# Two linear attentions behind a gate: B queries of the last two tiles moved into the key part, kv fed two tiles at a time, zeros on TensorE at the start, W buffers in another order

## The chip, the cores and the metric

One Trainium2 chip, one core of it. The metric is the device time of one execution in microseconds (us), as the median of several executions. TensorE is PE in the profile, with its weight loads in a row of their own (PEld); VectorE is DVE, ScalarE is ACT, GpSimd is POOL, and SP issues the DMAs.

## What is computed

Both attentions read the same x (2048 rows of 576), with 32 heads of 18 columns. A uses elu-like features, B a learned map per head and two softmaxes over 18 columns; neither is causal. A gate per row mixes the two.

```python
def reference(A_x, A_wqkv, A_wo, B_x, B_wqkv, B_w_phi, B_wo, gate_w):
    x = A_x
    g = sigmoid((x * gate_w).sum(-1, keepdims=True))
    # A: q, k, v from x @ A_wqkv, phi(t) = where(t > 0, t + 1, exp(t)) + 1e-6
    #    kv = einsum("bhsd,bhse->bhde", phi(k), v);  z = phi(k) summed over s
    #    a  = (phi(q) kv) / (phi(q) z + 1e-6) @ A_wo
    # B: q, k, v from x @ B_wqkv, pq = q w_phi per head, pk = k w_phi per head
    #    phi_q = concat([softmax(pq), softmax(-pq)]), phi_k likewise, then as in A with B_wo
    return g * a + (1 - g) * b
```

All is f32. The kernel keeps that accuracy by splitting each operand into a high and a low part in fp32r and multiplying three of the four products.

## The kernel before

The 2048 rows are 16 tiles of 128. A projection of a tile (`proj`, L157) is 14 matmuls of 288 columns for each half of the 576 columns: 4 full k-tiles with three products each, and the last 64 rows with their low parts packed into two matmuls. Results go to two-bank PSUM tiles named pq or to one-bank tiles named tr, two buffers of each name. Two more banks, named bk, hold the sums kv[0] and kv[1] over all key tiles, and later the output sums.

The work runs in four parts.

- Loads and folding of weights. A weight takes one of five W buffers; raw pieces come by DMA through wraw buffers (and, at the start, uw ones), ACT rounds them to the high part (L115) and DVE or POOL makes the low part (L117). The per-head map of B is folded into its key and query weights (`fold_w`, L142).
- The key part, over tiles 0 to 15: v of A (`do_v`), k of A with its feature map (`do_ak`, L173 to L175), k of B with its two softmaxes (`do_bk`: maximum and minimum L180 and L181, subtractions L187 and L188, exponential L189, sums L191, scaling L198), v of B, and the sums kv (L212): 11 small matmuls of A and 11 of B for each tile, fed with the features of the tile before. v stands in two buffers (vo).
- The transition: kv is masked into tiles (kt), z is summed out of it (L520 for B), A's kv is multiplied with A's output weight into MA (L348, L351, evacuated at L354), and B's kv is placed into kb_h and kb_l (L533, L537). Into this are woven the query units of tiles 14 and 15.
- The query loop, in blocks of two tiles in the order 14, 15, 0 to 13. For a tile, `q_units` projects B's query (the softmax steps as in `do_bk`, without the scaling), then A's with two gate columns more (L173 to L175, and gg = 1 + exp(-+gate), L366), then `norm_a` (L371 to L377) and `norm_b` (L384 to L392, scaling L198) apply denominators and gate; `tr_units` transposes the features (L428, L435, L440, L442) and splits them (L423, L424); `num` multiplies B's features with kb (L460, split at L465); `out_units` makes the output (L490).

The order of instructions on each engine isn't that of the code: a scheduler with a timeline of its own moves them, within the limits set by data and buffers. Each engine then takes its list strictly in order. All loads and stores wait in one list, on SP.

Of the kernel before, what the change touches and what calls it, by code (L numbers as in the profile page):

```python
# [1 line left out]

# [12 lines left out]
P = 128  # L15
# [13 lines left out]
def tile_gated_mix(ctx, tc, xT, wAk, wAv, wBv, wAq, wkT, wqT, phi, woA, woB, out):  # L29
# [68 lines left out]
    def load_x(t, eng=G):  # L98
        raw = wk.tile([P, 640], F32, name="xraw")
        nc.sync.dma_start(raw, xT[t].rearrange("p j n -> p (j n)"))  # L100
        raw = raw.rearrange("p (j n) -> p j n", n=P)
        xh = wk.tile([P, KT, P], F32R, name="xh")
        xl = wk.tile([P, KT, P], F32R, name="xl")
        A.activation(xh, raw, AF.Copy)  # L104
        eng.tensor_tensor(xl, raw, r(xh), op=ALU.subtract)  # L105
        return xh, xl
# [91 lines left out]
        eng.tensor_tensor(u3, u3, rs[:, :, None].to_broadcast([P, 64, DH]), op=ALU.mult)  # L198
# [102 lines left out]
    kv_b(t0, u0)
# [9 lines left out]
    for k in range(2):
        pz = tr_tile()
        w = min(324, D - 324 * k)
        for i in range(3):
            n = min(108, w - 108 * i)
            PE.matmul(pz[:, 108 * i:108 * i + n], sel_z, kta[3 * k + i][:, P:P + n], start=True, stop=True)
        A.activation(z_a[:, 324 * k:324 * k + w], pz[:, :w], AF.Copy)

    WoB = w_tile()
    for g in range(4):
        split(woB[:, g, :], WoB[:126, g, :D], WoB[:126, 5 + g, :D], G)
    raw = wraw_tile()[:96, :D]
    nc.sync.dma_start(raw, woB[:96, 4, :])
    A.activation(WoB[:64, 4, :D], raw[:64], AF.Copy)
    A.activation(wob_y[:64], raw[:64], AF.Copy)
    A.activation(wob_y[64:96], raw[64:96], AF.Copy, scale=tcol[64:96])
    G.tensor_tensor(wob_x[:96], raw[:96], r(wob_y[:96]), op=ALU.subtract)
    MA = w_tile()  # L330
# [30 lines left out]
    def maps_a(pa):  # L361
        f = phi_elu(pa)
        gg = sm.tile([P, 2], F32, name="gg")
        for i, sgn in enumerate((-1.0, 1.0)):
            A.activation(gg[:, i:i + 1], pa[:, 1, HB:HB + 1], AF.Exp, scale=sgn)
        V.tensor_scalar(gg, gg, 1.0, None, op0=ALU.add)  # L366
# [28 lines left out]

    qs = {}

    def q_units(t, x=None):
        x = x or load_x(t)
# [16 lines left out]
    def tr_units(t, at, uwt, tiles=(tr_tile, tr_tile)):
        f, uw = qs.pop(t)
# [81 lines left out]
        while seqs:  # L499
            seqs = [s for s in seqs if next(s, "end") != "end"]  # L500

    qu0, qu1, mau = q_units(t0, x0), q_units(t1, x1), ma_units()
    for _ in range(2):
        next(qu0)
    kv_b(t1, u1)


    for p, kt in enumerate(ktb):
        b, o = b_region(p)
        for a, m, n in widths(p):  # L510
            rows, c = slice(64 * a, 64 * a + m), P + 54 * a
            V.tensor_tensor(kt[rows].rearrange("p (s c) -> p s c", s=2)[:, :, c:c + n],
                            kv[b][rows, o:o + 2 * n].rearrange("p (s c) -> p s c", s=2),
                            mask[rows, a, None, :n].to_broadcast([m, 2, n]), op=ALU.mult)
        if p % 2 == 0:
            pz = tr_tile()
        n = min(108, D - 108 * p)
        for s in range(2):
            o = 216 * s + 108 * (p % 2)
            PE.matmul(pz[:, o:o + n], sel_z, kt[:, 320 * s + P:320 * s + P + n], start=True, stop=True)  # L520
# [3 lines left out]
        if p == 0:  # L524
            continue
        g, nh = GROUPS[p - 1]
        n, w = nh * DH, (nh * DH if g < 4 else 80)
        pk = tr_tile()
        for s in range(2):
            for c0, c1, base in [(0, n, 0)] + ([(72, 80, 64)] if g == 4 else []):  # L530
                for q in (g, p):
                    off = P + 126 * g - 108 * q
                    PE.matmul(pk[:n, 126 * s + c0:126 * s + c1], ktb[q][:, 320 * s + off:320 * s + off + n],  # L533
                              place[:, off + base:off + base + c1 - c0], start=(q == g), stop=(q == p))
        pkv = pk[:n, :252].rearrange("p (s c) -> p s c", s=2)[:, :, :w]
        A.activation(kb_h[:n, 2 * g:2 * g + 2, :w], pkv, AF.Copy)
        V.tensor_tensor(kb_l[:n, 2 * g:2 * g + 2, :w], pkv, r(kb_h[:n, 2 * g:2 * g + 2, :w]), op=ALU.subtract)  # L537
# [93 lines left out]
```

## Time and profile before

| | us |
|---|---|
| median of 3 executions | 625.88 (625.6 to 626.61) |
| the profiled execution | 623.18 |
| its span (first to last instruction) | 621.5 |

Busy time in the profiled execution, share of the span and instructions:

```profile
PE 604.0 (97%) x5000; PEld 591.5 (95%) x5000; DVE 391.5 (63%) x644; ACT 204.7 (33%) x420; POOL 174.4 (28%) x126
```

The median lies 2.7 us above the profiled execution; changes are counted on the profile and then carried over to the median. Rows of a timeline give the start, the time from there to the end, the engine, the line, the operation, output<-inputs and the number of records; a wait and what ended it stand in brackets. Ends of matmuls are modelled and overlap, so that pace is read from starts. An fp32 matmul leaves two records, an fp32r one leaves one. Rows of groups give the busy us of the group, the mean ns of one, and the idle us ahead of it.

### The profile page before, as it was taken

What the parts mean: (1) busy time and instruction counts of PE and PEld (TensorE: products, weight loads), DVE (VectorE), ACT (ScalarE), POOL (GpSimd) and SP (SyncE); (2) the same over time, 40 slices, a digit from 0 to 9 for tenths busy, and PEclk for the clock granted to TensorE, in tenths of its full rate; (3) what the DMA queues carried; (4) which work ended last, traced back from release to release, by engine and by line L of the source; (5) the groups of instructions that cost most, each with busy time, mean ns of one, the idle gap of its engine ahead of it and who ended that gap; (6) DMA issues with size and microseconds to landing.
All of it is one profiled execution on the core that took longest, in us unless ns stands there. A gap on an engine that the chain in (4) does not pass through costs nothing.

```text
span 621.5 us, 11676 instructions
## 1 busy us (share of the span) xinstructions
PE 604.0 (97%) x5000; PEld 591.5 (95%) x5000; DVE 391.5 (63%) x644; ACT 204.7 (33%) x420; POOL 174.4 (28%) x126
## 2 busy tenths in 40 slices
PE   6999999999999999999998799999999999999997
PEld 6999999999999999999997599999999999999997
DVE  6373353323323332326999998989889988889920
ACT  6342232221222222235333344243332334332331
POOL 6013221112222222245245212434133443312300
PEclk9999999999999999999999999999999999999999
DMA  8441130000000000024011101011010110000001
GB/s 285 124 142 41 44 112 3 21 22 22 22 22 24 22 22 24 22 64 122 22 38 50 35 22 40 22 42 41 20 41 22 41 42 20 20 20 20 16 24 39
DMA packets 12660, 27.94 MB, mean 45 GB/s; under 512 B 1388, under 2 KB 1388, under 8 KB 12608
## 3 DMA queue, kind: packets, MB, share of 16 engines
q1 hardware_dynamic: 12608, 27.19, 14.1%
q8 instruction: 39, 0.64, 0.4%
q14 instruction: 13, 0.11, 0.1%
HBM read 22.47 MB, written 4.72 MB: 44 GB/s over the span
## 4 chain that ended last, share of the span: by engine, by line
PE 82%; DVE 13%; ACT 2%; DMA 2%; issue 1%; SPq 0%; ACTq 0%
PE pq L157 32%; PE tr L157 19%; PE bk L490 16%; PE bk L212 5%; PE tr L460 4%; PE tr L435 2%; DVE row L384 1%; DVE dd L385 1%; DMA wraw<-wBv 1%; DVE uw L198 1%; PE tr L428 1%; DVE W L424 1%; PE pq L142 1%; DVE gg L366 1%; DVE row L175 1%; DVE den L373 1%
## 5 line engine op out<-in xcount | busy, mean ns | idle before, releaser
L157 PE MATMUL pq<-W,xh 128*128 128x288 f32 (+1 forms) x1152 | 254.3, 300 | 0.2 <-DVE den L390 0.2
L157 PEld LDWEIGHTS pq<-W,xh 128*128 128x128 f32 x1152 | 190.9, 189 | 3.1 <-PE tr L348 0.6
L157 PE MATMUL pq<-W,xl 128*128 128x288 f32 (+1 forms) x640 | 187.1, 298 | 0.0
L157 PE MATMUL tr<-W,xh 128*128 128x288 f32 x576 | 124.4, 301 | 5.8 <-ACT W L115 5.3
L105 POOL TENSOR_TENSOR xl<-xraw,xh 128x640 fp32r<-128x640 f32 x29 | 45.4, 1566 | 301.2 <-ACT xh L104 300.6
L157 PEld LDWEIGHTS pq<-W,xl 128*128 128x128 f32 x640 | 120.8, 189 | 0.2
L157 PEld LDWEIGHTS tr<-W,xh 128*128 128x128 f32 x576 | 96.7, 193 | 6.6 <-ACT W L115 5.3
L157 PE MATMUL tr<-W,xl 128*128 128x288 f32 x320 | 93.9, 299 | 0.0
L174 DVE TENSOR_SCALAR row<-row 128x576 f32<-128x576 f32 x32 | 24.4, 762 | 101.2 <-ACT row L173 101.2
L233 ACT ACTIVATE vo<-tr 128x288 f32<-128x288 f32 x64 | 25.9, 407 | 150.2 <-PE tr L157 150.2
L490 PE MATMUL bk<-W,ath 128*128 128x288 f32 x288 | 63.5, 301 | 1.1 <-ACT ath L423 0.7
L191 DVE TENSOR_REDUCE ss<-uw 128x64 f32<-128x1152 f32 x32 | 43.2, 1351 | 31.0 <-ACT uw L189 30.9
L157 PEld LDWEIGHTS tr<-W,xl 128*128 128x128 f32 x320 | 61.8, 193 | 0.0
L490 PE MATMUL bk<-W,vo 126*128 126x288 f32 x384 | 61.3, 299 | 0.0
L490 PEld LDWEIGHTS bk<-W,vo 126*128 126x128 f32 x384 | 54.0, 189 | 0.0
L180 DVE TENSOR_REDUCE mm<-pq 128x32 f32<-128x576 f32 x32 | 23.9, 748 | 47.0 <-PE pq L157 47.0
L189 ACT ACTIVATE uw<-uw 128x1152 f32<-128x1152 f32 x32 | 37.3, 1167 | 41.7 <-DVE uw L188 41.0
L490 PEld LDWEIGHTS bk<-W,ath 128*128 128x128 f32 x288 | 47.2, 189 | 1.5 <-ACT ath L423 0.9
L490 PE MATMUL bk<-W,atl 128*128 128x288 f32 x160 | 47.4, 297 | 0.0
L371 POOL TENSOR_TENSOR row<-row,z_a 128x576 f32<-128x576 f32 x16 | 30.1, 1882 | 52.5 <-DVE row L175 52.5
L460 PE MATMUL tr<-W,kb_h 126*126 126x256 f32 (+1 forms) x160 | 32.4, 283 | 1.0 <-DVE vo L465 0.8
L198 POOL TENSOR_TENSOR uw<-uw,rs 128x1152 f32<-128x1152 f32 x15 | 32.3, 2155 | 0.7 <-DVE rs L193 0.7
(138 smaller groups left out, 875.7 us busy)
## 6 DMA issues: line engine op xcount, KB each, us to landing
xraw<-xT SPq DMA_DIRECT2D x30, 320.0 KB, 3.1
out<-row SPq DMA_DIRECT2D x16, 288.0 KB, 2.1
wraw<-woA SPq DMA_DIRECT2D x6, 288.0 KB, 2.9
wraw<-wAq SPq DMA_DIRECT2D x5, 289.0 KB
wraw<-wBv SPq DMA_DIRECT2D x5, 288.0 KB, 4.2
wraw<-wkT SPq DMA_DIRECT2D x4, 315.0 KB
wraw<-wqT SPq DMA_DIRECT2D x4, 315.0 KB
uw<-wAk SPq DMA_DIRECT2D x4, 288.0 KB
```

The source lines that it names most:

```text
L105: eng.tensor_tensor(xl, raw, r(xh), op=ALU.subtract)
L157: PE.matmul(dst, xx[:, j, :], W[:, w, c0:c0 + n], start=(i == 0), stop=(i == len(steps) - 1))
L174: V.tensor_scalar(fx, fx, 1.0, EPS, op0=ALU.min, op1=ALU.add)
L180: V.tensor_reduce(mm[:, :32], heads(pq), op=ALU.max, axis=AX.X)
L189: A.activation(uw, uw, AF.Exp)
L191: V.tensor_reduce(ss, uw.rearrange("p s (h d) -> p (s h) d", d=DH), op=ALU.add, axis=AX.X)
L198: eng.tensor_tensor(u3, u3, rs[:, :, None].to_broadcast([P, 64, DH]), op=ALU.mult)
L212: PE.matmul(dst, vt[t % 2][:, which, 3 * gr:3 * gr + nh, :].rearrange("p h d -> p (h d)"), rhs, start=(t == 0 and first), stop=(t == NT - ...
L233: A.activation(vt[t % 2][:, which, 16 * hf:16 * hf + 16, :DH], pv[:, :HB].rearrange("p (h d) -> p h d", d=DH), AF.Copy)
L371: G.tensor_tensor(zw, f[:, :D], z_a, op=ALU.mult)
L460: PE.matmul(dst, kk[:n, i, :w], uu[:n, i, :256], start=(m == 0), stop=(m == 5))
L490: PE.matmul(po[:, :HB], l, w, start=(i == 0), stop=(i == len(steps) - 1))
```

## The change

It has five parts.

1. At the very start, DVE sets 128x288 elements to zero, and PE multiplies them five times in fp32, into a bk bank that nothing reads.
2. v stands in four buffers (two named ath, two vo), and `kv_pair` feeds kv with two tiles at once: A of both, then B of both, at every even tile.
3. B's query projection and softmax of tiles 14 and 15 (`q_b`) are taken out of `q_units` and put into the key part; their `norm_b` follows after both A queries. `fold_a` is the former code as a function, B's kv is folded in two loops instead of one, and the kt tiles are made later. The first two units of MA are woven with tile 15's `q_b`.
4. gg + 1 is done by ACT instead of DVE; tile 15's key scaling of B by POOL instead of DVE.
5. MA takes its W buffer ahead of WoB, so that MA gets the one that WAk leaves and WoB that of WBk.

```diff
+    warm = row_tile()[:, :HB]
+    V.memset(warm, 0.0)
+    pw = bank_tile()
+    for _ in range(5):
+        PE.matmul(pw[:, :HB], warm[:, :P], warm, start=True, stop=True)
...
-    for i in range(2):
-        v = wk.tile([P, 2, H, VC], F32, name="vo")
+    for i in range(4):
+        if i < 2:
+            v = wk.tile([P, 2, 640], F32, name="ath").rearrange("p a c -> p (a c)")[:, :2 * H * VC]
+            v = v.rearrange("p (a h d) -> p a h d", a=2, d=VC)
+        else:
+            v = wk.tile([P, 2, H, VC], F32, name="vo")
...
+    def kv_pair(pend):
+        for t, f, _ in pend:
+            kv_a(t, f)
+        for t, _, u in pend:
+            kv_b(t, u)
+        pend.clear()
...
-        if pend[0] is not None:
-            kv_a(t - 1, pend[0])
-        kv_b(t - 1, pend[1])
+        if t % 2 == 0:
+            kv_pair(pend)
...
-        V.tensor_scalar(gg, gg, 1.0, None, op0=ALU.add)
+        A.activation(gg, gg, AF.Copy, bias=1.0)
...
-    qu0, qu1, mau = q_units(t0, x0), q_units(t1, x1), ma_units()
-    for _ in range(2):
-        next(qu0)
+    do_v(t0, x0, WAv, 0)
+    f0 = do_ak(x0)
+    kv_pair(pend)
...
+    u0 = do_bk(x0)
+    do_v(t0, x0, WBv, 1)
+    weave(q_b(t0, x0, qb))
+    do_v(t1, x1, WAv, 0)
+    f1 = do_ak(x1)
+    kv_a(t0, f0)
+    kv_b(t0, u0)
...
+    WAq = load_w(wAq, 578, G)
+    u1 = do_bk(x1)
+    kv_a(t1, f1)
+    fold_a()
+    MA = w_tile()
+    WoB = w_tile()
...
+    mau = ma_units()
+    do_v(t1, x1, WBv, 1)
+    weave(q_b(t1, x1, qb), islice(mau, 2))
     kv_b(t1, u1)
...
-    weave(qu0, mau)
-    weave(qu1)
+    weave(mau, q_a(t0, x0, qa), q_a(t1, x1, qa))
+    for t in (t0, t1):
+        norm_b(*qb[t], qa[t][1])
+        qs[t] = (qa[t][0], qb[t][0])
```

How the instructions stand now, at three places. Names carry the number of their buffer, and line numbers of the changed kernel are a few higher or lower than before (L160 is the projection, L220 the kv sums, L183 and L184 maximum and minimum, L352 to L354 the denominator of A, L363 and L364 the products and sums with z of B, L562 the low part of kb).

PE's list at the start of the program, before (tr are the two halves of tile 0's v of A):

```order
L157 MATMUL tr_140<-W_115,xh_108 128x288
L157 MATMUL tr_156<-W_115,xh_108 128x288
L157 MATMUL tr_140<-W_115,xh_108 128x288
L157 MATMUL tr_140<-W_115,xl_109 128x288
L157 MATMUL tr_140<-W_115,xh_108 128x288
```

and now:

```order
L66 MATMUL bk_72<-row_70 128x288 x5
L160 MATMUL tr_148<-W_123,xh_116 128x288
L160 MATMUL tr_164<-W_123,xh_116 128x288
L160 MATMUL tr_148<-W_123,xh_116 128x288
L160 MATMUL tr_148<-W_123,xl_117 128x288
```

The five products of zeros (row) stand ahead of the first projection, which is as it was.

PE's list in the middle of the key part, at one feeding of kv, before (row are features of A, uw those of B, vo is v):

```order
L157 MATMUL pq_2308<-W_204,xl_2178 128x288
L212 MATMUL bk_104<-row_2171,vo_102 57x54 x10
L212 MATMUL bk_104<-row_2171,vo_102 38x36
L212 MATMUL bk_104<-uw_2235,vo_102 57x108 x2
L212 MATMUL bk_105<-uw_2235,vo_102 57x108 x8
L212 MATMUL bk_105<-uw_2235,vo_102 38x72
L157 MATMUL pq_2369<-W_298,xh_2177 128x288 x2
```

and now:

```order
L160 MATMUL pq_2290<-W_212,xl_2182 128x288
L220 MATMUL bk_112<-row_1987,vo_108 57x54 x10
L220 MATMUL bk_112<-row_1987,vo_108 38x36
L220 MATMUL bk_112<-row_2175,vo_110 57x54 x10
L220 MATMUL bk_112<-row_2175,vo_110 38x36
L220 MATMUL bk_112<-uw_2073,vo_108 57x108 x2
L220 MATMUL bk_113<-uw_2073,vo_108 57x108 x8
L220 MATMUL bk_113<-uw_2073,vo_108 38x72
L220 MATMUL bk_112<-uw_2217,vo_110 57x108 x2
L220 MATMUL bk_113<-uw_2217,vo_110 57x108 x8
L220 MATMUL bk_113<-uw_2217,vo_110 38x72
L160 MATMUL pq_2373<-W_295,xh_2181 128x288 x2
```

One stretch now feeds two tiles. Over the whole program the kv matmuls stood in 22 stretches between other matmuls, and stand in 17.

DVE's list in the transition, around the maximum and minimum of B's query of tile 0 (mm), before:

```order
L385 TENSOR_REDUCE dd_3201<-row_3202 128x32
L537 TENSOR_TENSOR kb_l_97<-tr_3119,kb_h_96 72x2x80
L384 TENSOR_TENSOR row_3346<-uw_3289,z_b_95 128x576
L366 TENSOR_SCALAR gg_3330<-gg_3330 128x2
L387 TENSOR_TENSOR dd_3201<-dd_3201,rs_3049 128x64
L180 TENSOR_REDUCE mm_3401<-pq_3365 128x32
L181 TENSOR_REDUCE mm_3401<-pq_3365 128x32
L385 TENSOR_REDUCE dd_3342<-row_3346 128x32
L389 SCALAR_TENSOR_TENSOR den_3209<-dd_3201 128x32
```

and now:

```order
L354 RECIPROCAL den_3318<-den_3318 128x32
L183 TENSOR_REDUCE mm_3415<-pq_3379 128x32
L184 TENSOR_REDUCE mm_3415<-pq_3379 128x32
L190 TENSOR_TENSOR uw_3418<-pq_3379,mm_3415 128x576
L191 TENSOR_TENSOR uw_3418<-mm_3415,pq_3379 128x576
L363 TENSOR_TENSOR row_3346<-uw_2818,z_b_99 128x576
L364 TENSOR_REDUCE dd_3342<-row_3346 128x32
L364 TENSOR_REDUCE dd_3342<-row_3343 128x32
L194 TENSOR_REDUCE ss_3422<-uw_3418 128x64
L363 TENSOR_TENSOR row_3360<-uw_3111,z_b_99 128x576
L562 TENSOR_TENSOR kb_l_101<-tr_3171,kb_h_100 126x252
```

The products with z_b of tiles 14 and 15 and all of kb_l stood ahead of tile 0's maximum, and now follow it. From the loop's first output matmuls on, PE's list is as it was. On SP's list the load of woA's last piece stood ahead of that of tile 5's x, and now stands behind it.

More of the change, by code (lines that the diff above doesn't have):

```diff
@@ L1 @@
 from contextlib import ExitStack
+from itertools import islice
 import concourse.bass as bass
@@ L211, in kv_group @@
     def kv_group(t, which, gr, nh, dst, rhs, first):
-        PE.matmul(dst, vt[t % 2][:, which, 3 * gr:3 * gr + nh, :].rearrange("p h d -> p (h d)"), rhs,
+        PE.matmul(dst, vt[t % 4][:, which, 3 * gr:3 * gr + nh, :].rearrange("p h d -> p (h d)"), rhs,
                   start=(t == 0 and first), stop=(t == NT - 1), skip_group_check=True)
@@ L258, in tile_gated_mix @@
     f1 = do_ak(xs[1])
-    kv_a(0, f0)
     WBk = fold_w(wkT)
@@ L264, in tile_gated_mix @@
     xs[2] = load_x(2)
-    kv_a(1, f1)
     u1 = do_bk(xs[1])
-    kv_b(0, u0)
     do_v(1, xs.pop(1), WBv, 1)
-    pend = (None, u1)
+    pend = [(0, f0, u0), (1, f1, u1)]
     for t in range(2, NT - 2):
@@ L311, in tile_gated_mix @@
[L311 to L330, printed above, removed]
+    def fold_a():
+        for p, kt in enumerate(kta):
+            for a, m, n in widths(p):
+                rows, c = slice(64 * a, 64 * a + m), P + 54 * a
+                V.tensor_tensor(kt[rows, c:c + n], kv[0][rows, 54 * p:54 * p + n], mask[rows, a, :n], op=ALU.mult)
+        for k in range(2):
+            pz = tr_tile()
+            w = min(324, D - 324 * k)
+            for i in range(3):
+                n = min(108, w - 108 * i)
+                PE.matmul(pz[:, 108 * i:108 * i + n], sel_z, kta[3 * k + i][:, P:P + n], start=True, stop=True)
+            A.activation(z_a[:, 324 * k:324 * k + w], pz[:, :w], AF.Copy)
@@ L409, in q_units @@
         proj(pa[:, 1, :HB + 2], x, WAq, HB, HB + 2)
-        sa = maps_a(pa)
-        norm_a(*sa)
-        qs[t] = (sa[0], sb[0])
+        qs_a[t] = maps_a(pa)
+        norm_a(*qs_a[t])
         yield
-        norm_b(*sb, sa[1])
+    def q_units(t, x=None, qb=None):
+        x = x or load_x(t)
+        if qb is None:
+            qb = {}
+            yield from q_b(t, x, qb)
+        qa = {}
+        yield from q_a(t, x, qa)
+        qs[t] = (qa[t][0], qb[t][0])
+        norm_b(*qb[t], qa[t][1])
+        yield
     def tr_units(t, at, uwt, tiles=(tr_tile, tr_tile)):
@@ L500, in weave @@
             seqs = [s for s in seqs if next(s, "end") != "end"]
-    qu0, qu1, mau = q_units(t0, x0), q_units(t1, x1), ma_units()
-    for _ in range(2):
-        next(qu0)
+    t0, t1 = NT - 2, NT - 1
+    x0 = xs.pop(t0)
+    qa, qb = {}, {}
+    do_v(t0, x0, WAv, 0)
+    f0 = do_ak(x0)
+    kv_pair(pend)
+    kts = [wk.tile([P, 2, 640], F32, name=n) for n in ("ath", "atl", "ath", "atl")]
+    kta = [kts[p // 4].rearrange("p a c -> p (a c)")[:, 320 * (p % 4):320 * (p % 4) + 320] for p in range(NPAIR)]
+    for kt in kts:
+        G.memset(kt, 0.0)
+    xs[t1] = x1 = load_x(t1)
+    u0 = do_bk(x0)
[5 more added lines that the diff above has]
+    kv_b(t0, u0)
+    ktx = wk.tile([P, 2, 640], F32, name="vo")
+    G.memset(ktx[:, 0], 0.0)
+    ktb = [kts[1][:, 1], kts[2][:, 0], kts[2][:, 1], kts[3][:, 0], kts[3][:, 1], ktx[:, 0]]
+    WAq = load_w(wAq, 578, G)
[4 more added lines that the diff above has]
+    WoB = w_tile()
+    for g in range(4):
+        split(woB[:, g, :], WoB[:126, g, :D], WoB[:126, 5 + g, :D], G)
+    raw = wraw_tile()[:96, :D]
+    nc.sync.dma_start(raw, woB[:96, 4, :])
+    A.activation(WoB[:64, 4, :D], raw[:64], AF.Copy)
+    A.activation(wob_y[:64], raw[:64], AF.Copy)
+    A.activation(wob_y[64:96], raw[64:96], AF.Copy, scale=tcol[64:96])
+    G.tensor_tensor(wob_x[:96], raw[:96], r(wob_y[:96]), op=ALU.subtract)
+    mau = ma_units()
+    do_v(t1, x1, WBv, 1)
+    weave(q_b(t1, x1, qb), islice(mau, 2))
     kv_b(t1, u1)
@@ L514, in tile_gated_mix @@
                             mask[rows, a, None, :n].to_broadcast([m, 2, n]), op=ALU.mult)
+    for p, kt in enumerate(ktb):
         if p % 2 == 0:
@@ L523, in tile_gated_mix @@
             A.activation(z_b[:, :, k:k + 108 + n], pz[:, :432].rearrange("p (s c) -> p s c", s=2)[:, :, :108 + n], AF.Copy)
-        if p == 0:
-            continue
-        g, nh = GROUPS[p - 1]
+    for g, nh in GROUPS:
+        p = g + 1
         n, w = nh * DH, (nh * DH if g < 4 else 80)
@@ L537, in tile_gated_mix @@
         V.tensor_tensor(kb_l[:n, 2 * g:2 * g + 2, :w], pkv, r(kb_h[:n, 2 * g:2 * g + 2, :w]), op=ALU.subtract)
-    weave(qu0, mau)
-    weave(qu1)
+    weave(mau, q_a(t0, x0, qa), q_a(t1, x1, qa))
+    for t in (t0, t1):
+        norm_b(*qb[t], qa[t][1])
+        qs[t] = (qa[t][0], qb[t][0])
     def at_tiles():
```

36 lines of the change are left out of this document (5 added, 31 removed).

## The prediction

> **What bounds the kernel now.** I read the windows first: busy time of each engine by stage. The columns are the window, its length, then busy us (and records) of PE, PEld, DVE, ACT and POOL, the granted clock, the DMA share and GB/s.
>
> ```profile
> 100.00:267.00 167.00, 167.00 (x1545) 164.34 (x1545) 58.70 (x80) 39.79 (x70) 36.74 (x20) 1.00 0.07 21
> 309.00:360.00 51.00, 44.51 (x314) 39.62 (x313) 48.62 (x91) 19.67 (x46) 19.91 (x14) 1.00 0.13 38
> 360.00:570.00 210.00, 209.94 (x1621) 209.70 (x1621) 187.92 (x316) 75.83 (x170) 69.39 (x44) 1.00 0.09 29
> 570.00:622.00 52.00, 46.58 (x354) 45.33 (x352) 23.46 (x41) 15.11 (x35) 4.77 (x3) 1.00 0.08 30
> ```
>
> In the key part (100 to 267) and the query loop (360 to 570) PE is never idle: there only fewer or cheaper matmuls gain. In the transition (309 to 360) DVE is busy 48.62 of 51 us and PE has 6.5 us free: DVE is the bound. The list of PE's waits (engine, tile and line, waited for, us in total, times, longest) says where PE stands still:
>
> ```profile
> PE tr L157 <- ACT W L115: 5.3, 1, 5.3
> PE bk L435 <- DVE uw L198: 3.8, 1, 3.8
> PE tr L348 <- DVE W L354: 1.3, 1, 1.3
> PE tr L460 <- DVE vo L465: 0.8, 1, 0.8
> ```
>
> The 5.3 is the first load. The 3.8 and 1.3 lie in the transition (with 0.4 behind L357 and a small one, 5.7 in all), the 0.8 in the tail.
>
> **The start: zeros on TensorE.** The timeline of the first us:
>
> ```profile
> 9.30 0.79 DVE L117 TENSOR_TENSOR W<-uw,W 64x576 fp32r<-64x576 f32 x1
> 9.65 0.69 PE L157 MATMUL tr<-W,xh 128*128 128x288 f32 x2
> 10.29 0.69 ACT L115 ACTIVATE W<-uw 128x576 fp32r<-128x576 f32 x1 [0.25 <-DMA uw<-wAk]
> 10.37 0.69 PE L157 MATMUL tr<-W,xh 128*128 128x288 f32 x2
> 12.20 0.69 PE L157 MATMUL pq<-W,xh 128*128 128x288 f32 x3
> ```
>
> From 9.65 to 10.37 PE issues three matmuls (two here, one xl between): 0.24 us each. Later the same shape goes every 0.14 (290.65 to 290.79, quoted below). The page's row of granted clocks shows full speed all along, so the spacing has to be read instead. The first projection ends at 12.20 because it runs at half pace until about 11.6, not for want of operands: its last weight piece is there at 10.09 (9.30 + 0.79), and the next one (WAk's first, on ACT) at 10.98. If PE is at full pace when it starts, the first pq matmul moves from 12.20 to 10.98: **1.2 us** gained. I take all of it, since PE then stays busy with pieces that came before they were needed. Bounds: 0 if the zeros change nothing, and a loss of 0.7 if they also hold PE past 5.33: five fp32 matmuls at the slow pace, begun once the memset is through, take to about 6.0 (an estimate: two passes each, as the two records of an fp32 matmul elsewhere suggest, and a slower pass than 0.24).
>
> [...]
>
> **The key part: kv in pairs.** Breaks in the projection stream cost more than their matmuls:
>
> ```profile
> 112.24 0.29 PE L157 MATMUL pq<-W,xl 128*128 128x288 f32 x1
> 114.63 0.29 PE L157 MATMUL pq<-W,xl 128*128 128x288 f32 x1
> 282.40 0.29 PE L157 MATMUL tr<-W,xl 128*128 128x288 f32 x1
> 283.72 0.30 PE L157 MATMUL pq<-W,xl 128*128 128x288 f32 x1
> 290.65 0.30 PE L157 MATMUL tr<-W,xh 128*128 128x288 f32 x1
> 290.79 0.29 PE L157 MATMUL tr<-W,xl 128*128 128x288 f32 x1
> 292.57 0.30 PE L157 MATMUL pq<-W,xl 128*128 128x288 f32 x1
> ```
>
> From 112.24 to 114.63 lie one kv_a and one kv_b together, from 282.40 to 283.72 a kv_a alone, from 290.79 to 292.57 a kv_b alone; each interval holds three projection matmuls besides (3 x 0.14 = 0.4). So joined 2.0, apart 0.9 + 1.4 = 2.3: a join saves 0.3. The order has 22 stretches of kv matmuls before and 17 after. 5 x 0.3 = **1.5 us**, bounds 1.0 and 1.9. PE is the only busy engine there, so nothing hides it. Scaling tile 15's uw on POOL instead of DVE and moving memsets costs nothing while POOL works 36.74 of 167 us.
>
> **The transition.** Two B query projections with their softmax work leave it, and the folding of B's kv (L520, L533, L537) comes later.
>
> ```profile
> 303.48 1.04 PE L520 MATMUL tr<-ath,row 128*128 128x108 f32 x8
> 304.35 1.06 PE L533 MATMUL tr<-row,ath 128*126 128x126 f32 x8
> 305.16 0.38 PE L157 MATMUL pq<-W,xh 128*128 128x288 f32 x1
> 320.98 1.13 PE L348 MATMUL tr<-wraw,ath 128*128 128x288 f32 x4
> 321.73 0.64 PE L157 MATMUL pq<-W,xh 128*128 128x288 f32 x2
> 324.23 0.75 DVE L180 TENSOR_REDUCE mm<-pq 128x32 f32<-128x576 f32 x1
> 351.94 1.35 DVE L198 TENSOR_TENSOR uw<-uw,rs 128x1152 f32<-128x1152 f32 x1
> 354.54 0.66 PE L428 MATMUL tr<-ident,row 128*128 128x128 f32 x4 [0.38 <-ACT W L357]
> ```
>
> Take as marker tile 0's B query projection: PE ends it at 320.98, DVE takes it (L180) only at 324.23, and 27.7 us of gapless DVE work later stands a scaling (L198), behind which PE begins the loop's transposes at 354.54. By the order, PE passes the marker earlier: 24 L533 products now stand behind it (four take 0.81, the last groups are smaller, so about 4.2) and 8 of the 12 L520 products (1.7), while four pairs of L348 move ahead of it (0.75 to 0.9 each, 3.0 to 3.6). Net 2.3 to 2.9, and DVE has less before it, so it takes the marker at once: about 319 on the old clock. What its list from there to the scaling gains and loses, in a view of DVE's groups from 309 to 355 (busy us, mean ns, idle):
>
> ```profile
> L384 DVE TENSOR_TENSOR row<-uw,z_b 128x576 f32<-128x576 f32 x3 | 4.4, 1459 | 0.0
> L385 DVE TENSOR_REDUCE dd<-row 128x32 f32<-128x576 f32 x6 | 4.3, 735 | 0.0
> L354 DVE TENSOR_TENSOR W<-tr,W 128x288 fp32r<-128x288 f32 x8 | 3.5, 439 | 0.0
> L373 DVE TENSOR_REDUCE den<-row 128x32 f32<-128x576 f32 x3 | 2.2, 744 | 0.0
> L366 DVE TENSOR_SCALAR gg<-gg 128x2 f32<-128x2 f32 x3 | 1.7, 561 | 0.0
> L537 DVE TENSOR_TENSOR kb_l<-tr,kb_h 126x252 fp32r<-126x252 f32 (+1 forms) x4 | 1.5, 383 | 0.0
> L374 DVE TENSOR_SCALAR den<-den,gg 128x32 f32<-128x32 f32 x3 | 1.0, 328 | 0.0
> L375 DVE RECIPROCAL den<-den 128x32 f32<-128x32 f32 x4 | 1.3, 332 | 0.0
> ```
>
> Added: five L537 (1.9), two L384 (2.9), two L385 (1.5), a small product of dd (0.2, as tiny ops here). Removed: four L354 (1.8), two L366 now on ACT (1.1), one L373, L374 and L375 (1.4). Net 6.5 - 4.3 = 2.2 (1.4 if the L384 take the 0.74 that they take without POOL beside them, 3.3 if all added ones stretch). So the scaling comes at 319 + 27.7 + 2.2 = 348.9 and the transposes at 351.5: **3.0 us**. Bounds: 0, if DVE takes the marker no earlier, and 5.7, all the waits. What is late next is PE's wait for a scaled uw and for a pq buffer that DVE holds: some 2 to 3 us remain.
>
> The moved gg ops cost ACT 16 short ops in a loop where it works 75.83 of 210 us, nothing. The W order puts WoB's loads behind the last key projection with WBk, which ends ahead of the fold (303.48); WoB is first needed behind the transposes at 354.54. Some 50 us hide loads that took a few us each, and a cover that thick needs no price. On SP's queue woA's last piece stands behind tile 5's x, at most 1 us on a load of 2.9, used last of the L348 stretch: nothing.
>
> **The tail.**
>
> ```profile
> 578.32 2.21 POOL L371 TENSOR_TENSOR row<-row,z_a 128x576 f32<-128x576 f32 x1 [9.75 <-DVE row L175]
> 579.15 1.40 DVE L366 TENSOR_SCALAR gg<-gg 128x2 f32<-128x2 f32 x1
> 582.05 0.68 DVE L465 TENSOR_TENSOR vo<-tr,vo 126x512 fp32r<-126x512 f32 x1
> 582.79 0.34 PE L460 MATMUL tr<-W,kb_h 72*80 72x256 f32 x1 [0.75 <-DVE vo L465]
> ```
>
> PE waits 0.75 for a DVE op that stands behind gg, two columns wide and yet 1.40 us long, beside POOL's op. With gg on ACT the wait goes: **0.75**, bounds 0 and 1.1.
>
> [...]
>
> **Sum.** 1.2 + 1.5 + 3.0 + 0.75 = 6.45. The profiled execution took 623.18 (span 621.5, 1.7 around it), so it would take 616.7. The median of three is 625.88, 2.7 above it; from there, **619.4**.
>
> **Rivals.**
> A, the forecast: 619.4, own range 617.5 to 621. For it: DVE's list and marker. Chance 0.50.
> B, the transition loses all its waits, since DVE comes into its worst stretch with two softmaxes already done: 5.7 for 3.0, so 616.7. Against it: DVE's list still grows. 0.17.
> C, DVE stays as late, because norm_b of both tiles (L384 and L385 above, 8.7 us with tile 0's) now comes in one lump with the fold: the transition gains nothing, 622.4. 0.14.
> D, the zeros wake nothing, or end too late: without 1.2 and with 0.7 more, 621.3. 0.06.
> Between C and E, no change: the lump eats the other gains, about 625. 0.07.
> E, slower: the late fold of B makes DVE a longer chain than now. Its eight small ops beside POOL's products (L369, L353, L371 of the new kernel's lines) each wait as gg did, 1.40 for some 0.25: 8 x 1.15 = 9.2 us, less 6.45, so 628.6. It decides from 6.45 on, and is slower by a readable amount from 7.7. Against it: in the transition gg has a mean of 561 ns, so one op in three meets POOL's. 0.06.
>
> **How the numbers follow.** About 0.2%, 1.25 us, can be told from no change: faster means under 624.6. A, B, C and D are: 0.87; same 0.07; slower 0.06. The range takes in B and C with the bounds of the start and of the joins: 615.6 to 623.8. What is left out is mostly E and the near-zero case.
>
> **What would show it.** Matmuls 0.14 apart from the first projection on, and the first pq matmul near 11.0. Stretches of 88 kv records every two tiles. PE's waits between fold and loop down to 2 or 3 us, named behind DVE for pq and uw. No wait at L465's successor in the tail. The forecast is wrong if the transition's span does not shrink, or if the slow spacing is still there after the first weights have come.

## The result, and the profile after

The changed kernel has a median of 620.59 us (620.34 to 621.41, four executions) against 626.25 us (625.6 to 627.23, four) before: a ratio of 0.9911, 95% interval 0.9893 to 0.9928. That is 5.7 us less. The two profiled executions differ by half of it: 618.6 us of span against 621.5. Where the other half is, is the main question below.

Busy time by stage in the changed kernel's profile (columns as before: window, length, then PE, PEld, DVE, ACT, POOL, granted clock, DMA share, GB/s):

```profile
100.00:267.00 167.00, 167.00 (x1558) 165.67 (x1557) 58.73 (x80) 39.78 (x70) 39.02 (x22) 1.00 0.07 21
309.00:360.00 51.00, 46.18 (x321) 41.51 (x320) 46.54 (x88) 19.11 (x48) 20.26 (x14) 0.93 0.12 33
360.00:570.00 210.00, 210.00 (x1623) 210.00 (x1622) 178.74 (x308) 78.55 (x182) 67.68 (x43) 1.00 0.09 29
```

The same two stages are full of matmuls. In the transition PE is idle for 4.8 us instead of 6.5, but the clock column, 1.00 before, reads 0.93. Line numbers of the changed kernel from here on: L108 is the former L105 (low part of x), L201 the former L198 (scaling), L327 and L333 the former L348 and L354 (MA), L345 the former L366 (gg), L413 the former L424 (split), L417 and L424 the former L428 and L435 (transposes), L454 the former L465. PE's longest waits:

```profile
PE tr L327 <- DVE den L353: 3.2, 1, 3.2
PE bk L66 <- DVE row L63: 1.3, 1, 1.3
PE pq L160 <- ACT gg L344: 0.8, 1, 0.8
```

The waits of 5.3 (start, where PE now multiplies zeros from 1.28 us on) and 0.8 (tail) are gone; so are the 3.8 and the 1.3 of the transition, but a 3.2 and a 0.8 (for a pq buffer) stand in their place. At the start the timeline shows:

```profile
6.32 0.29 PE L160 MATMUL tr<-W,xl 128*128 128x288 f32 x1
6.45 0.43 PE L160 MATMUL tr<-W,xh 128*128 128x288 f32 x2
10.86 0.54 PE L160 MATMUL pq<-W,xh 128*128 128x288 f32 x2
11.24 0.82 PE L160 MATMUL tr<-W,xh 128*128 128x288 f32 x4
```

Matmuls stand 0.13 us apart at 6.3 us already, and the first pq matmul is at 10.86 where it was at 12.20. Behind two pq matmuls PE now goes on with the 28 of another tr projection; before, eight pq matmuls stood there.

The new wait, in the timelines of DVE, of POOL and of PE:

```profile
332.72 1.70 DVE L201 TENSOR_TENSOR uw<-uw,rs 128x1152 f32<-128x1152 f32 x1
...
337.46 2.68 DVE L201 TENSOR_TENSOR uw<-uw,rs 128x1152 f32<-128x1152 f32 x1
340.06 0.31 DVE L562 TENSOR_TENSOR kb_l<-tr,kb_h 72x160 fp32r<-72x160 f32 x1
```

```profile
337.07 1.86 POOL L108 TENSOR_TENSOR xl<-xraw,xh 128x640 fp32r<-128x640 f32 x1 [3.87 <-ACT xh L107]
```

```profile
336.18 1.13 PE L327 MATMUL tr<-wraw,ath 128*128 128x288 f32 x4
340.52 2.26 PE L327 MATMUL tr<-wraw,ath 128*128 128x288 f32 x4 [3.20 <-DVE den L353]
```

The second L327 row needs one of the two tr buffers, and by the order its buffer is the one that the last group of kb had: it comes free when DVE has made kb_l (340.06 + 0.31 = 340.37). The wait is put down to L353, which only happened to end next; PE starts 0.15 us behind kb_l, and in a_pool (below) the view puts waits of L327 down to kb_l itself. DVE had been busy with the scalings of tiles 14 and 15, one of them 2.68 us long beside POOL's L108 where such a scaling took 1.35 before. The row at 340.52 then takes twice the time of the one at 336.18, and the windows around it say why:

```profile
335.95:339.36 3.41, 1.37 (x7) 0.81 (x6) 3.41 (x4) 1.88 (x5) 1.86 (x1) 1.00 0.00 0
339.36:346.19 6.83, 5.67 (x16) 4.29 (x17) 6.74 (x15) 1.94 (x5) 2.55 (x2) 0.50 0.32 91
346.19:349.60 3.41, 3.41 (x25) 3.20 (x24) 2.98 (x11) 1.28 (x6) 0.13 (x1) 1.00 0.00 0
```

For 6.83 us PE ran at a granted clock of 0.50.

### The profile page after: what moved, and what is told of

Read it like the earlier page. It is cut to its first block, busy times and chain, and to the rows that moved or that the text cites. A ratio compares the mean times of both kernels' runs of the same rounds, so it can differ in the third digit from the quotient of the medians.

```text
span 618.6 us, 11647 instructions
## 1 busy us (share of the span) xinstructions
PE 606.8 (98%) x5010; PEld 593.5 (96%) x5010; DVE 377.6 (61%) x628; ACT 207.3 (34%) x436; POOL 176.2 (28%) x130
## 4 chain that ended last, share of the span: by engine, by line
PE 86%; DVE 6%; DMA 3%; ACT 2%; POOL 1%; issue 1%; SPq 0%; DVEq 0%; ACTq 0%; POOLq 0%
PE pq L160 33%; PE bk L479 19%; PE tr L160 18%; PE tr L449 4%; PE bk L220 4%; PE tr L424 2%; PE tr L327 1%; DMA wraw<-woB 1%; PE tr L417 1%; POOL W L120 1%; DMA wraw<-wAv 1%; PE pq L145 1%; DMA wraw<-wBv 1%; DVE uw L201 1%; PE tr L145 1%
## 5 line engine op out<-in xcount | busy, mean ns | idle before, releaser
L160 PE MATMUL pq<-W,xh 128*128 128x288 f32 (+1 forms) x1152 | 253.8, 300 | 0.8 <-ACT gg L344 0.8
L160 PEld LDWEIGHTS pq<-W,xh 128*128 128x128 f32 x1152 | 190.9, 189 | 2.6 <-ACT gg L344 1.1
L160 PE MATMUL pq<-W,xl 128*128 128x288 f32 (+1 forms) x640 | 186.6, 297 | 0.0
L108 POOL TENSOR_TENSOR xl<-xraw,xh 128x640 fp32r<-128x640 f32 x29 | 45.8, 1581 | 284.3 <-ACT xh L107 281.8
L160 PE MATMUL tr<-W,xh 128*128 128x288 f32 x576 | 122.6, 298 | 1.5 <-ACT ath L248 0.8
L160 PEld LDWEIGHTS pq<-W,xl 128*128 128x128 f32 x640 | 120.9, 189 | 0.5 <-issue 0.4
L160 PEld LDWEIGHTS tr<-W,xh 128*128 128x128 f32 x576 | 94.8, 189 | 3.1 <-ACT ath L248 1.0
L160 PE MATMUL tr<-W,xl 128*128 128x288 f32 x320 | 92.5, 295 | 0.0
L194 DVE TENSOR_REDUCE ss<-uw 128x64 f32<-128x1152 f32 x32 | 43.3, 1352 | 31.8 <-ACT uw L192 31.8
L160 PEld LDWEIGHTS tr<-W,xl 128*128 128x128 f32 x320 | 60.4, 189 | 0.0
L183 DVE TENSOR_REDUCE mm<-pq 128x32 f32<-128x576 f32 x32 | 23.8, 745 | 51.5 <-PE pq L160 51.5
L350 POOL TENSOR_TENSOR row<-row,z_a 128x576 f32<-128x576 f32 x16 | 29.0, 1813 | 54.8 <-DVE row L178 51.1
L248 ACT ACTIVATE vo<-tr 128x288 f32<-128x288 f32 x32 | 13.0, 407 | 85.2 <-PE tr L160 85.2
L201 POOL TENSOR_TENSOR uw<-uw,rs 128x1152 f32<-128x1152 f32 x16 | 34.4, 2152 | 9.5 <-DVE rs L196 9.5
L248 ACT ACTIVATE ath<-tr 128x288 f32<-128x288 f32 x32 | 12.9, 406 | 66.9 <-PE tr L160 66.9
```

The costliest lines, as they stand in the source:

```text
L160: PE.matmul(dst, xx[:, j, :], W[:, w, c0:c0 + n], start=(i == 0), stop=(i == len(steps) - 1))
L183: V.tensor_reduce(mm[:, :32], heads(pq), op=ALU.max, axis=AX.X)
L194: V.tensor_reduce(ss, uw.rearrange("p s (h d) -> p (s h) d", d=DH), op=ALU.add, axis=AX.X)
L248: A.activation(vt[t % 4][:, which, 16 * hf:16 * hf + 16, :DH], pv[:, :HB].rearrange("p (h d) -> p h d", d=DH), AF.Copy)
L350: G.tensor_tensor(zw, f[:, :D], z_a, op=ALU.mult)
```

## The experiments

Each trace is compared at the same matmul of the program, so that only time differs, not the work. The table gives how many us earlier than in the second trace of the kernel before (b_again, below) four such points are reached: the 113th projection matmul (31.3 us there), the 561st (106.3), the 1625th (268.0, kv of the same tiles done), an output matmul in the loop (490.6) and the last output matmul (620.3). From these come the terms: joins is the change from 106 to 268, transition that from 268 to 490, tail that from 490 to the end. One execution each.

| kernel | 31 | 106 | 268 | 490 | end | joins | transition | tail | ratio to before (95%) |
|---|---|---|---|---|---|---|---|---|---|
| before, first trace | 0.2 | 1.4 | 1.4 | 2.6 | 2.6 | 0 | 1.2 | 0 | |
| b_zeros | 1.4 | 2.5 | 2.5 | 2.7 | 2.6 | 0 | 0.2 | 0 | 0.9977 (0.9966 to 0.9987) |
| b_gg | -0.1 | -0.1 | -0.1 | -1.2 | 0.3 | 0 | -1.1 | 1.4 | 0.9997 (0.9985 to 1.001) |
| changed kernel, first trace | 1.2 | 2.2 | 3.8 | 4.1 | 5.4 | 1.6 | 0.3 | 1.4 | 0.9911 (0.9893 to 0.9928) |
| a_again, the same | 0.6 | 1.3 | 2.9 | 2.1 | 3.5 | 1.6 | -0.8 | 1.4 | 0.9927 (0.9913 to 0.994) |
| a_nozeros | 0.1 | 0.8 | 2.4 | 3.2 | 4.6 | 1.6 | 0.7 | 1.4 | 0.9937 (0.9925 to 0.995) |
| a_qback | 1.0 | 2.6 | 4.2 | 4.4 | 5.7 | 1.6 | 0.1 | 1.4 | 0.9915 (0.9901 to 0.993) |
| a_ggdve | 0.4 | 1.2 | 2.8 | 4.5 | 4.4 | 1.6 | 1.7 | 0 | 0.992 (0.9906 to 0.9935) |
| a_single | 0.6 | -0.8 | -0.8 | -0.1 | 1.2 | 0 | 0.6 | 1.4 | 0.9946 (0.9925 to 0.9967) |
| a_mix | 1.2 | 2.4 | 4.0 | 5.7 | 7.1 | 1.6 | 1.7 | 1.4 | 0.9894 (0.9882 to 0.9907) |
| q_mix | 1.4 | 1.6 | 3.3 | 2.2 | 3.6 | 1.6 | -1.1 | 1.4 | 0.9942 (0.993 to 0.9954) |
| a_pool | 0.9 | 2.6 | 4.2 | 3.5 | 4.9 | 1.6 | -0.7 | 1.4 | 0.9934 (0.9919 to 0.9948) |
| q_pool | 0.6 | 1.8 | 3.4 | 0.5 | 1.9 | 1.6 | -2.9 | 1.4 | 0.997 (0.9955 to 0.9986) |

Two columns are the same in every kernel that has the edit and zero in every other: joins and tail. Three others move, and the experiments go after them.

**The zeros alone, and all but the zeros.**

```diff
 # a_nozeros: the changed kernel; b_zeros adds the same five lines to the kernel before
-    warm = row_tile()[:, :HB]
-    V.memset(warm, 0.0)
-    pw = bank_tile()
-    for _ in range(5):
-        PE.matmul(pw[:, :HB], warm[:, :P], warm, start=True, stop=True)
```

> The changed kernel without the zeros on TensorE. Theory (the zeros raise the pace before the first projection, and 1.0 of the 1.3 us is kept behind the weight loads): the first matmuls are 0.24 us apart again, the first pq matmul stands near 12.2 instead of 10.86, and the time is 1.0 us over the changed kernel's (621.6 where that has 620.6). Rival (loads set the pace behind the first tile, so the gain is lost by 30 us): within 0.3 us of the changed kernel.

> The kernel before with the zeros alone. Theory: 1.0 us faster than before, with the early pace of 0.13 us from the first products that follow the zeros. Rival (the gain needs the later kv of the changed kernel beside the folding of weights): under 0.4 us.

Without the zeros the changed kernel took 621.56, 1.0 us more than its 620.59, which was measured in another series (by the ratios to before, 0.9937 against 0.9911 and 0.9927, it is 0.6 to 1.6); with them the kernel before took 624.34, 1.1 us less than the 625.43 of the same series. At 31 us the traces are 1.1 us apart in the one case and 1.4 in the other. The size of the theory holds in both kernels, and the gain doesn't need the rest of the change.

The mechanism that it names is only half of it, for the five lines change PE's list too. In all traces with the zeros two pq matmuls stand behind the first projection and then 28 others, in all without them eight pq matmuls. And in the second trace of the kernel before (b_again), which has no zeros, matmuls were 0.13 us apart from 9.9 us on, the first trace reaching this pace only at 11.8:

```profile
11.23 0.42 PE L157 MATMUL pq<-W,xh 128*128 128x288 f32 x2
12.50 0.40 PE L157 MATMUL pq<-W,xh 128*128 128x288 f32 x1 [0.84 <-DVE W L117]
```

There the first pq matmul came 1.0 us earlier, and the third waited for its weights and stood at 12.50, where the first trace has it at 12.48. So with the old list the earlier pace earned nothing; the gain comes from the zeros with the list that came with them. Over all traces the first pq matmul stands at 10.77 to 11.77 us with the zeros and at 11.23 to 12.46 without, which overlaps, but the 57th projection matmul at 14.80 to 15.76 with them and at 16.05 to 16.21 without. What the list would give without the zeros, no run shows.

**gg on ACT alone.**

```diff
 # b_gg: the kernel before
-        V.tensor_scalar(gg, gg, 1.0, None, op0=ALU.add)
+        A.activation(gg, gg, AF.Copy, bias=1.0)
```

> The kernel before with gg + 1 on ACT alone. Theory (the stall behind the two-column op is the whole of the tail's gain): 0.8 to 1.4 us faster, PE's 0.75 us wait near 582 gone. Rival one (the stall passes to the next DVE op): within 0.3 us. Rival two (the op also held DVE up in the transition): 2 to 4 us faster, PE's waits of 3.8 and 1.3 us there shorter.

The median is 625.23 against 625.43: no difference. The trace says that this is no zero of its own but a sum: 1.4 gained in the tail, 1.1 lost in the transition (against b_again; 2.3 against the first trace of before). So the stall is the tail's, as the first theory has it, and a price that nobody expected stands against it elsewhere.

**B queries of tiles 14 and 15 put back.**

```diff
 # a_qback: the changed kernel
-    weave(q_b(t0, x0, qb))
...
-    weave(q_b(t1, x1, qb), islice(mau, 2))
+    qu0, qu1 = q_units(t0, x0), q_units(t1, x1)
+    for _ in range(2):
+        next(qu0)
...
-    weave(mau, q_a(t0, x0, qa), q_a(t1, x1, qa))
-    for t in (t0, t1):
-        norm_b(*qb[t], qa[t][1])
-        qs[t] = (qa[t][0], qb[t][0])
+    weave(qu0, mau)
+    weave(qu1)
```

> The changed kernel with the B queries of tiles 14 and 15 back behind the key part, all else as changed. Theory of the record (moving them gains 3.0 us in the transition): 3 us slower than the changed kernel, about 623.6. Rival (by the trace PE loses 1.3 us in the transition of the changed kernel: its 3.2 us wait for a PSUM buffer behind two scalings and the late kb_l is new): 1 to 2 us faster than the changed kernel, about 619, without that wait.

619.92, a ratio of 0.9915 where the changed kernel has 0.9911 and, in another series, 0.9927: taken out of the changed kernel, its largest move is worth nothing that can be told. PE's longest waits in this trace:

```profile
PE tr L327 <- DVE W L333: 1.8, 2, 1.4
PE tr L559 <- DVE kb_l L563: 1.6, 2, 1.1
PE bk L424 <- DVE uw L201: 1.5, 1, 1.5
```

They are more than the changed kernel's, but spread; none is over 1.5 us, and the clock stayed at 1.00 all through.

**The kernel before, once more.**

> The kernel before, unchanged, for a second trace. Of its 23 timed executions those with a granted clock of 0.994 had a mean of 626.2, those with 1.000 623.8, and the first trace (623.18) is one of the latter. Theory (PE's 3.8 us wait lets the clock fall, and half pace behind it costs 2 to 3 us): this trace, if below 1.000, is the same as the first up to that wait, shows a granted clock near 0.5 for some 5 us from about 345 on, and its loop starts 2 to 3 us later. Rival (the variation lies in the loads or in the launch): the shift is there ahead of 300, or the spans agree and only the time around them differs.

Its timed executions lay with those of before (ratio 1.0003, 0.9991 to 1.0016). The trace has the same instructions as the first one, and is 2.6 us longer, in two places. 1.4 of it is there by 106 us, in waits that the first trace doesn't have or has shorter. The longest of them:

```profile
PE tr L157 <- ACT vo L233: 0.9, 1, 0.9
...
PE pq L142 <- DMA wraw<-wqT: 0.6, 1, 0.6
```

The wait for wqT, near 90 us, is new; that for v, near 44 us, was 0.5 in the first trace; 0.4 lies ahead of it, half of that in the wait for wkT (0.34 for 0.15). The 0.84 at 12.50 us isn't among them, since it only uses up the early pace.

The other 1.2 comes behind the 3.8 us wait for tile 14's scaled uw, which both traces have. Windows of 3.41 us, of the second trace and then of the first:

```profile
344.04:347.45 3.41, 1.27 (x8) 1.09 (x8) 3.32 (x8) 0.98 (x2) 0.39 (x1) 1.00 0.34 108
347.45:350.87 3.42, 3.42 (x11) 2.46 (x10) 3.42 (x8) 1.43 (x6) 2.20 (x2) 0.50 0.00 0
```

```profile
339.45:342.86 3.41, 1.46 (x8) 0.90 (x6) 3.41 (x7) 1.58 (x3) 1.54 (x1) 1.00 0.32 87
342.86:346.27 3.41, 1.53 (x9) 1.16 (x9) 3.32 (x9) 0.98 (x2) 0.65 (x1) 1.00 0.32 96
346.27:349.68 3.41, 3.34 (x21) 2.81 (x21) 3.41 (x8) 1.38 (x6) 1.96 (x2) 1.00 0.00 0
```

In the second trace the wait left PE 1.27 us of work in one window (and 1.73 in the one ahead of it, 340.63 to 344.04), and the next ran at a granted clock of 0.50; in the first the same wait left it 1.46 and 1.53 us in two windows, and the clock stayed at 1.00. So the theory (a wait, then low clock) and the rival (loads) each have about half. Of the 65 executions of the kernel before in the three series of these experiments, three show a mean granted clock of 1.000: the first trace, which has it too, is the rare case, and the median, 2.7 us above it, the usual one.

**The scalings of tiles 14 and 15 on POOL.**

```diff
 # a_pool: the changed kernel; q_pool: the same on a_qback
-        scale_uw(uw, rs, V)
+        scale_uw(uw, rs, eng)
...
-        norm_b(*qb[t], qa[t][1])
+        norm_b(*qb[t], qa[t][1], G)
```

> The changed kernel with the scalings of tiles 14 and 15 in norm_b on POOL instead of DVE. Theory (DVE's two scalings of 1.7 and 2.7 us stand ahead of the last kb_l, and PE's new 3.2 us wait is for the buffer that it frees): that wait goes, the clock stays up, 2 to 3 us faster than the changed kernel, about 618. Rival (PE only waits later, for the scaled uw, which POOL makes in 2.15 instead of 1.35 us): within 0.7 us of the changed kernel.

> The changed kernel with the B queries of tiles 14 and 15 back behind the key part (which took 619.9), and with the scalings of these tiles in norm_b on POOL. Theory (DVE is the bound of the transition): 1 to 2 us faster than without the second edit, about 618.4. Rival (POOL is as late as DVE): 619.5 to 620.5.

Both are misses: 0.9934 and 0.997, worse than without the edit (for a_pool by little against the changed kernel's second ratio, 0.9927). In a_pool the wait for kb_l did shrink (1.2 us in two parts, where it was 3.2), and POOL had both tiles scaled by 337.3; but a new wait came behind it:

```profile
PE bk L424 <- DVE W L413: 2.4, 1, 2.4
```

L424, the next transposes, needs a bk buffer that DVE empties with the split of tile 14's transposes (L413), and in this order DVE does that at 342.35. So neither side had it right: relieving DVE of two operations moved PE's wait to another operation of DVE, and a_pool, 0.4 us ahead of the changed kernel's trace at 268 us, is 0.6 behind it in the loop.

**gg back on DVE, everywhere or early only.** a_ggdve takes back the edit of b_gg in the changed kernel; the other two split it by tile.

```diff
 # a_mix: the changed kernel; q_mix: the same on a_qback; early is t >= t0 or t < 2
-        A.activation(gg, gg, AF.Copy, bias=1.0)
+        if early:
+            V.tensor_scalar(gg, gg, 1.0, None, op0=ALU.add)
+        else:
+            A.activation(gg, gg, AF.Copy, bias=1.0)
```

> The changed kernel with gg + 1 back on DVE. Theory (the tail's gain, 1.4 us between the traces, comes from gg on ACT): 1 to 1.4 us slower than the changed kernel, with the 0.75 us wait of PE near the end. Rival (by the kernel before with gg on ACT, which was 0.2 us faster only, the gg move is worth nothing): within 0.4 us.

> The changed kernel with gg + 1 on DVE for tiles 14, 15, 0 and 1 and on ACT for the others. Theory (by the traces gg on ACT gains 1.4 us in the tail and loses 1.0 to 1.9 in the transition, where the order on DVE and ACT shifts with it): both are kept, 0.7 to 1.4 us faster than the changed kernel. Rival (what was lost in the transition is one more window of low clock, by chance): within 0.4 us.

> The changed kernel with the B queries of tiles 14 and 15 back behind the key part and gg + 1 on DVE for tiles 14, 15, 0 and 1. Theory: as the edit before, 0.7 to 1.4 us faster than the same without it (0.9915 of before). Rival: within 0.4 us of it.

With gg on DVE everywhere the tail's 1.4 are gone, and the transition is 1.4 better than in the changed kernel's first trace (2.5 better than in a_again): 621.22, a ratio of 0.992 between the changed kernel's two, so no difference, by a sum again. With gg on DVE for the first four tiles only, both are kept: **619.31 us, 0.9894, 1.85 us under the changed kernel's 621.16 of the same series**, the fastest here and faster than both kernels. DVE and PE at the place of the new wait, in a_mix:

```profile
333.99 1.34 DVE L201 TENSOR_TENSOR uw<-uw,rs 128x1152 f32<-128x1152 f32 x1
...
337.74 1.34 DVE L201 TENSOR_TENSOR uw<-uw,rs 128x1152 f32<-128x1152 f32 x1
339.01 0.31 DVE L565 TENSOR_TENSOR kb_l<-tr,kb_h 72x160 fp32r<-72x160 f32 x1
```

```profile
339.47 1.21 PE L327 MATMUL tr<-wraw,ath 128*128 128x288 f32 x4 [2.13 <-DVE den L356]
```

Both scalings take 1.34 us, where they took 1.70 and 2.68: POOL's operations end before they begin here (at 332.38 and 337.20), and in the changed kernel's trace ran beside them (to 333.20, and from 337.07 to 338.93); the wait is 2.13 instead of 3.20. All four traces with gg on ACT, the queries moved and the scalings on DVE (both of the changed kernel, a_nozeros, a_single) have the long scalings and the 3.2 us wait, and both with gg on DVE early (a_mix, a_ggdve) have neither. One window of low clock stays, behind one in which PE worked 1.23 us:

```profile
337.76:341.17 3.41, 1.23 (x5) 0.70 (x5) 3.38 (x8) 0.81 (x3) 0.00 (x0) 1.00 0.34 96
341.17:344.59 3.42, 3.42 (x11) 2.73 (x12) 3.39 (x8) 1.51 (x5) 2.28 (x2) 0.50 0.33 86
```

q_mix is a miss, 622.16. The four kernels are two edits crossed (for the changed kernel with gg on ACT throughout, both series):

| | gg early on DVE | gg on ACT |
|---|---|---|
| B queries moved | 0.9894 | 0.9911, 0.9927 |
| B queries put back | 0.9942 | 0.9915 |

With gg early on DVE the move of the queries is worth 0.0048 of 626, or 3.0 us; with gg on ACT nothing. What the one edit is worth depends on the other. Some of it lies outside the spans: an execution takes longer than its span by 1.70 to 1.77 us in a_mix, 1.67 to 1.79 in a_qback, 2.04 to 2.06 in q_mix and 2.04 to 2.15 in the changed kernel. These 0.3 us are part of the 3.0, and of a_mix's 1.85; they go with no single edit, and no row shows their cause.

**kv one tile at a time.**

```diff
 # a_single: the changed kernel
-        if t % 2 == 0:
-            kv_pair(pend)
+        kv_pair(pend)
```

> The changed kernel with kv fed one tile at a time in the loop over tiles 2 to 13, from the same four buffers. Theory (a break in the projections costs 0.3 us and five or six more stand here): 1.5 to 2.0 us slower than the changed kernel, the loss spread evenly, 0.33 us for two tiles. Rival (the breaks hide behind the weight loads): under 0.4 us.

623.62, 2.5 us over the changed kernel of the same series. Between 106 and 268 us it keeps its distance to the kernel before to the hundredth, where the paired kernels gain 0.33 us for two tiles, 1.64 in all. The rest of the 2.5 came early: in this trace PE waited 0.9 us for wqT, and a window of low clock followed:

```profile
PE pq L145 <- DMA wraw<-wqT: 0.9, 1, 0.9
```

```profile
90.90:94.31 3.41, 3.41 (x17) 3.41 (x16) 0.69 (x2) 0.42 (x2) 0.00 (x0) 0.50 0.34 87
```

Two of its six executions took only 620.33 and 620.90, so this early loss isn't in all of them.

Two parts of the change have no run of their own: the order of the W buffers, and tile 15's key scaling on POOL.

**a_again**, the changed kernel once more:

> The changed kernel, unchanged, for a second trace and more executions beside the three others of this call. Theory (what varies between executions are waits for loads before 90 us and how PE's 3.2 us wait lies in windows of 3.41 us of the clock): the same order of work, the clock at 0.50 for a whole number of 3.41 us, and a difference to the first trace that lies in these two places alone. Rival: it varies elsewhere too.

Its trace differs from the first in just these places: 0.9 us by 106 us, and 1.1 behind the 3.2 us wait, where again about 6.8 us ran at a granted clock of 0.50 (means of 0.76 from 340 to 345 us and of 0.56 from 345 to 350), but at another point of the work. In between and behind, to the end, the two agree to 0.04 us.

## Why the prediction came out right, and where it was wrong

The total was near (619.4 for 620.6) and inside the range, but not by its own sum: that it came so near is luck. The sum was to hold for the profiled executions, and between those it fell short: 2.9 us of span for 6.45. Point by point.

**The start: right in size, by a reason that was half of it.** 1.2 forecast; the first pq matmul stood at 10.86 for a forecast 10.98, and 1.0 to 1.1 us of it reached the median, shown by taking the zeros away and by adding them alone. Rival D is out. But "PE then stays busy with pieces that came before they were needed" doesn't hold for the list of before, where b_again's early pace was lost to a wait of 0.84 us; it holds for the list that the zeros brought with them. And the 10.86 is one trace of a kernel whose other one has 11.58.

**The joins: right.** 1.5 forecast, 1.64 in all nine traces of kernels with pairs, 0 in the others.

**The transition: wrong.** The step that failed is "the scaling comes at 319 + 27.7 + 2.2 = 348.9". In the changed kernel's trace DVE takes the marker at 317.72 and makes that scaling at 349.55:

```profile
316.32 0.75 DVE L352 TENSOR_REDUCE den<-row 128x32 f32<-128x576 f32 x1 [1.17 <-POOL row L350]
...
317.72 0.69 DVE L183 TENSOR_REDUCE mm<-pq 128x32 f32<-128x576 f32 x1
...
349.55 1.35 DVE L201 TENSOR_TENSOR uw<-uw,rs 128x1152 f32<-128x1152 f32 x1
```

The marker is 1.1 us late against 319 less the 2.4 gained ahead of it: DVE didn't take it at once but stood idle for 1.17 us, waiting for a product of POOL's that L352, ahead of it in DVE's list, needs. The list behind the marker is 31.8 us long instead of the forecast 29.9. So the scaling is 2.39 us earlier than before, no more than was gained ahead. The two stretched scalings alone are 1.70 of the 1.9 us, where I had priced them at the 1.35 that they take with POOL idle. The other terms of the 2.2 were off too, and nearly cancel: the two products with z_b took 1.4 for 2.9 (that they take 0.74 each only without POOL beside them, as the prediction has it, no row shows: before's trace has one of 0.74 at 431.30, beside POOL's L371 of 2.22 us from 431.13 on), the two gg that left the list had taken 0.15 each there and not 0.55 (the long one, 1.38, stood ahead of the marker), and one product of dd took 1.26 for 0.2. In a_mix, without the stretch, the list is 30.4. Behind the scaling the transposes followed in 3.5 us, where it was 2.6; PE had not stood idle since its 3.2 us wait ended, and 5.67 us of that were at a granted clock of 0.50, so I put these 0.9 down to the clock, a cost that no step had. Between the marks at 268 and 490 us the changed kernel takes 222.3 us, the first trace of before 221.4: by its own sign ("wrong if the transition's span does not shrink") this step failed. The move itself is worth the forecast 3.0 us, but only where gg stays on DVE early (shown by the four crossed kernels), and the step that priced the moved gg at "nothing" is the other half of the error: it looked at the loop, and in the transition the move cost 1.1 or 2.3 us in the kernel before and 1.4 or 2.5 in the changed one, against either of their two traces.

Rival E had this mechanism, an operation of DVE that takes longer beside POOL's, but too high a price and, but for one, the wrong operations (of those that it named, an L369 took 1.05 us; such a row, L390 with 1.08, stood in the list before, too); C, "the transition gains nothing", is what the changed kernel's trace shows, but for another reason than its lump of norm_b. E's mechanism shows at the scaling that begins at 337.46, behind POOL's L108 (337.07, 1.86 us long): it takes 2.68 us, where it took 1.34 in a_mix, behind the end of that L108. So taking gg off DVE left the wait to the scalings in the transition, and not in the tail: there the operation that had stood behind gg, the reduction L364 (576.69), took 0.75 us beside POOL's L350 (575.74, 2.20 us), and had taken 0.74 before.

**The tail: right in kind, too small.** 0.75 forecast for the wait alone; 1.37 to 1.41 measured in all nine kernels with gg on ACT there, and none in the others. The row of gg and the next split:

```profile
575.96 0.20 ACT L345 ACTIVATE gg<-gg 128x2 f32<-128x2 f32 x1
```

```profile
578.65 0.68 DVE L454 TENSOR_TENSOR vo<-tr,vo 126x512 fp32r<-126x512 f32 x1
```

The split that PE had waited for is 3.40 us earlier (582.05 before), of which 1.47 were gained ahead of it; what PE gains beyond its 0.75 is in matmuls behind, where waits and breaks too small for the list went with it. That part I have only from the times, not from an experiment.

**From the profile to the median: wrong, and to the good.** "From there, 619.4" added 2.7 us as if it were the same for both kernels. It isn't. The first trace of before had neither the longer waits ahead of 90 us nor the window of low clock that b_again has, 2.6 us together. Against b_again the changed kernel's trace gains 5.43: 1.18 at the start, 0.98 in the loads behind it, 1.64 at the joins, 0.26 in the transition, 1.37 in the tail. This sum is near the medians' 5.7. It isn't all of it: around its span an execution takes 1.67 to 1.79 us in the kernel before, and 2.04 to 2.15 in the changed one, where the prediction kept 1.7. These 0.3 to 0.4 us are lost outside the spans, and between these two executions' times the gain is 5.0. So the transition's missing 2.7 us were made up by a median of before that carried costs its profile didn't show. The 0.98 of the loads varies from trace to trace of one kernel (0.67 in a_again, 1.2 between the two of before), and how much of it belongs to the change stays open.

## What to carry to other kernels

Before a profile is taken as the base of a sum, compare its own time with the median: where they differ by more than the terms at stake, get a second trace and see in which stages they part. An operation taken off an engine that waits beside another one doesn't always take its stall along (the gg of 1.38 us left the transition, and a scaling there took 2.68 for 1.34); look at what stands next on that engine while the other one works. Edits on a stretch where two engines wait for each other didn't add up here (one move was worth 3.0 us or nothing): cross them (both, each alone, neither) before a price is put on one.

## What the runs showed of the hardware

TensorE's granted clock read 0.50 from 339.36 to 346.19 us in the changed kernel's first trace (6.83 us), from 347.45 to 350.87 in b_again (3.42), from 341.17 to 344.59 in a_mix (3.42) and from 90.90 to 94.31 in a_single (3.41). In the 3.41 us ahead of these, all at 1.00, PE was busy for 1.37, 1.27, 1.23 and 2.52 us. In the first trace of before it was busy for 1.46 and then 1.53 us in two such windows, and the clock stayed at 1.00 in them and in the next. The length of a wait alone doesn't tell these apart: behind one of 2.13 us in a_mix the clock read 0.50, and behind one of 3.83 in the first trace of before 1.00. What does, no run shows. In the changed kernel's trace PE was busy for 2.25 us of the first 3.41 at 0.50, and the next 3.42 were at 0.50 too; in a_mix it was busy for all of the first 3.42, and the next 3.41 were at 1.00.

In b_again the 3.42 us at 0.50 cost 1.2 us, the difference of the two traces of before behind it. DVE was busy through all of it too and kept its pace (an L424 of 126x512 took 0.67 us there, and 0.67 to 0.68 in the first trace), so that it set part of the pace; that this is the reason is argued, not tested.
